# Cross-covariance attention with a highway layer: transposes of v in 32-bit words and by DMA, larger load groups, and a first chain that reads S in place

## The chip, the core and the metric

The kernel runs on one core of one Trainium2 chip. The metric is device time in microseconds (us), the median over runs; of the kernel before, three runs gave 270.11 us (270.1 to 270.67). A profile is one execution recorded by the hardware profiler. In it PE is TensorE (its matmuls), PEld its weight loads, DVE is VectorE, ACT is ScalarE, POOL is GpSimd and SP is SyncE.

## What is computed

`q`, `k`, `v` are four batches of 6336 rows by 256 channels in float32, and the output has the same 25344 x 256 values. Cut to what matters:

```python
qn = q / (np.linalg.norm(q, axis=1, keepdims=True) + 1e-06)     # norm of a channel over all 6336 rows
kn = k / (np.linalg.norm(k, axis=1, keepdims=True) + 1e-06)
s = kn.transpose(0, 2, 1) @ qn / tau                            # 256 x 256 per batch
a = np.exp(s - s.max(-1, keepdims=True)); a /= a.sum(-1, keepdims=True) + 1e-09
x = (v @ a).reshape(B * N, 256)
H = np.maximum(x @ w_h, 0.0)
T = 1.0 / (1.0 + np.exp(-(x @ w_t + b_t)))
out = T * H + (1.0 - T) * x
```

A batch's 256 x 256 matrix needs all rows of its q and k before the first row of its output can be made.

## The kernel before

**Tiles.** Of a batch's 6336 rows, 6272 are read as 49 tiles of 128 rows and the last 64 rows of all batches come as an extra tile ("rem"). GpSimd loads q, k and v in groups of several tiles (`QG`, `VG`; `load`, L177), cast to float16 on the way, into rings of 4 buffers for q, 4 for k and 3 for v. The very first four tiles of q and k come as float32 over SP and ACT and are cast by DVE and ACT (`cast_first`).

**Scores.** For each tile TensorE adds k^T q into the PSUM tile S (two matmuls of 256 columns, L230) and k^T k and q^T q, of which the diagonal is the squared norm, into G (two matmuls of 128 columns each, L234 and L239). For some runs of four tiles (`RUNS`) the squares are made instead by ACT (L449), POOL (L455) and DVE (L462), so those tiles need no G matmul. In the last `TAIL` tiles of a batch all of q's G matmuls come first, then k's, then S.

**The chain.** When a batch's scores are done, a chain of small steps makes its matrices (`make_chain`): norms from the diagonals (DVE, L503), roots, inverses, a copy of S from PSUM to SBUF on ACT (`ssb`, L520), the row `cq` of q's inverse norms spread over partitions by TensorE (L549), the product (DVE, L558), exp on ACT (L575), softmax (DVE, L589), a transpose (`at`, L600, copied at L611), and the products with w_h and w_t (`ah`, L619, copied at L630). Results lie side by side in `mr`: the attention matrix, and it times w_h and w_t. The chain of batch b runs while outputs of batch b-1 are being made; batch 0 has nothing to run beside it but the first scores of batch 1.

**Outputs.** The 25 pairs of tiles of each batch make 100 slots. A slot needs its v transposed: four TensorE transposes of 128 x 128 float16 into PSUM (`vtps`, L293) and one copy to SBUF (`vts`, L307) by DVE or ACT (`ACT_COPY`). Then come twelve matmuls of 256 columns at L317: four into `zbank` (the gate, onto a bias that ACT put there at L361), four into `h`, four into `x`. ACT makes the sigmoid `tt` (L358), DVE makes max(h,0)*tt (`o`, L366) and (tt-1)*x (`ux`, L376), POOL subtracts them (L399), and SP stores four slots at a time (L416).

**The order.** Every engine runs its instructions in order. The order is written by a planner inside the kernel: it steps through time with a length for each task, takes on each engine the first task of a list of queues that is ready, and emits it. Loads go out in the order of `order` when their buffer is free by the plan and at most `OUTST` are under way; stores are held back by `step_sp` while loads are waiting. `S_END` says by which slot the scores of the next batch are to be done.

Of the kernel before, what the change touches and what calls it, by code (L numbers as in the profile page):

```python
# [60 lines left out]
def kernel(  # L61
# [33 lines left out]
    QG = [spans(4, 8, 8, 8, 8, 8, 3, 2), spans(4, 4, 12, 12, 12, 5)]  # L95
    QG += [spans(4, 8, 12, 12, 8, 5)] * (B - 2)
    VG = [spans(4, 8, 12, 12, 13)] + [spans(12, 12, 12, 13)] * (B - 1)
    GT = {"q": 12, "k": 12, "v": 13}
    CH = 4
    SQR = {"q": 4, "k": 2}  # L100
    RUNS = {1: {'q': [4, 8, 20, 32, 36, 44], 'k': [0, 8, 24, 28, 32, 40]}, 2: {'q': [0, 8, 12, 16, 20, 24, 28, 36, 40], 'k': [0, 12, 16, 32, 40]}, 3: {'q': [8, 12, 20, 28, 32, 40, 44], 'k': [0, 8, 16, 28, 32, 36]}}
    TAIL = [6, 12, 10, 7]
    SPARE = 0
    QOFF, VOFF = [1.5, 3.0, 4.0, 0.5], [7.5, 3.5, 0.5, 9.5]
    SAHEAD = [0, 0.5, 10.0, 10.5]
    LOOKS = [3, 3, 2, 2]
    HOLD = [2, 1, 1, 5]
    DVE_SUBS = 3
    SINGLES = 8
    ACT_COPY = {3, 14, 21, 22, 26, 34, 36, 39, 40, 44, 45, 51, 53, 54, 58, 61, 63, 64, 72, 77, 81, 83, 84, 88, 91, 96, 98, 99}  # L110
    NEAR = 2
    OUTST = 7
    QRING, VRING, ORING = 4, 3, 7
    TTR, UXR, VTR = 4, 3, 5
    OG = 4
    LASTS_AT = 18
    LASTS = list(range(LASTS_AT)) + [NPAIR - 1] + list(range(LASTS_AT, NPAIR - 1))
    PAIRS = [list(range(NPAIR))] * (B - 1) + [LASTS]
    S_END = [21.5, 42.5, 65.0]
# [17 lines left out]
    for t in range(NSLOT):  # L137
        b, i = pair_of(t)
        if i % 2 == 1 and i < NPAIR - 1 and unit_of[t - 1][1] == 0 and t < NSLOT - SINGLES:
            pairsets[-1].append(t)  # L140
            unit_of[t] = (len(pairsets) - 1, 1)
        else:
            unit_of[t] = (len(pairsets), 0)
            pairsets.append([t])
# [9 lines left out]
    MM = lambda n: n / 2376.0 + 0.0025  # L154
    EXP_LAG = 0.6
    PE_LAG, LAG, TO_PE = 0.20, 0.08, 0.10
    TILE = 0.309
    STEP, LAND = 0.01, 0.9

# [10 lines left out]

    def load(kind, b, g):
        src = {"q": q, "k": k, "v": v}[kind]
        s0, ns = (VG if kind == "v" else QG)[b][g]
        ring = VRING if kind == "v" else QRING
        t = stream_pool.tile([P, GT[kind], C], f16, tag=f"{kind}_in", bufs=ring, name=f"{kind}{b}_{g}")
        tiles[kind, b, g] = t
        return nc.gpsimd.dma_start(out=t[:, 0:ns, :], in_=rows(src[b])[:, s0 : s0 + ns, :])  # L177
# [35 lines left out]
    S_t, G_t = {}, {}  # L213
# [5 lines left out]
    def emit_score(b, j, parts, first, last):  # L219
        if first:  # L220
            tags = ("S", "G") if b == 0 else ("hx1", "hx2")
            S_t[b] = psum_pool.tile([P, 2, C], f32, tag=tags[0], name=f"S{b}")
            G_t[b] = psum_pool.tile([P, 4, P], f32, tag=tags[1], name=f"G{b}")
        nr = REM if j == NS else P
        kk, qq = tile_of("k", b, j), tile_of("q", b, j)
        S, G = S_t[b], G_t[b]
        for c in range(2):
            kc = kk[0:nr, bass.ts(c, P)]
# [4 lines left out]
            if "k" in parts:  # L233
                nc.tensor.matmul(  # L234
                    G[:, c, :], kc, kc, start=begins(b), stop=False, skip_group_check=True,
                )
        for c in range(2 if "q" in parts else 0):
            qc = qq[0:nr, bass.ts(c, P)]
            nc.tensor.matmul(  # L239
                G[:, 2 + c, :], qc, qc, start=begins(b), stop=False, skip_group_check=True  # L240
# [4 lines left out]
    def begins(b):  # L245
        if b in begun:
            return False
        begun.add(b)
        return True
# [3 lines left out]
    def make_scores(b):  # L253
# [3 lines left out]
        for parts in "qks":  # L257
# [26 lines left out]
    vT_ps, vT_t = {}, {}  # L284
    slot_of = {pair_of(t): t for t in range(NSLOT)}

    def emit_transpose(t):
        b, i = pair_of(t)
        ps = psum_pool.tile([P, 2, 2, P], f16, tag="vT", name=f"vtps{t}")
        for u, r in enumerate(nrows(i)):  # L290
            vt = tile_of("v", b, 2 * i + u)
            for c in range(2):
# [3 lines left out]
        vT_ps[t] = ps  # L296

    def emit_copy(t, e):
        i = pair_of(t)[1]
        sb = work_pool.tile([P, 2, 2, P], f16, tag="vTs", bufs=VTR, name=f"vts{t}")  # L300
        cp = nc.vector.tensor_copy if e == "DVE" else nc.scalar.copy
        ps = vT_ps.pop(t)
        if i == NPAIR - 1:
            for u, r in enumerate(nrows(i)):
                cp(out=sb[:, u, :, 0:r], in_=ps[:, u, :, 0:r])
        else:
            cp(out=sb, in_=ps)  # L307
        vT_t[t] = sb
# [3 lines left out]
    def mains(t, dst, off, seeded):  # L312
        b, i = pair_of(t)
        mr = mr_t[b]
        for u, r in enumerate(nrows(i)):
            for kt in range(2):
                nc.tensor.matmul(  # L317
                    dst[0:r, u, :], vT_t[t][:, u, kt, 0:r], mr[:, kt, off : off + C],
# [14 lines left out]
    banks = [Bank("hx0")]  # L333
# [36 lines left out]

    def emit_ux(t):
# [10 lines left out]
    def out_tile(t):  # L382
# [3 lines left out]
        if i % OG == 0:  # L386
            o_t[b] = stream_pool.tile([P, 2 * OG, C], f32, tag="o", bufs=ORING, name=f"o{t}")
        return o_t[b], 2 * (i % OG)
# [43 lines left out]
    def make_run(kind, b, g, j):  # L432
# [37 lines left out]
        rd = Task(("red", kind, b, j), "DVE", 1.0, reduce, [(ad, LAG)])  # L470
        sq.after.append((task_of_load[kind, b, g], LAND))
# [21 lines left out]
    def make_chain(b):  # L493
        st = {}
        T = {}
        def norms(kind):
            def emit(e):
# [3 lines left out]
                for i in (o, o + 1):  # L501
                    junk = work_pool.tile([P, P], f32, tag="junk", bufs=1, name=f"junk{b}_{i}")
                    nc.vector.scalar_tensor_tensor(  # L503
                        out=junk, in0=G_t[b][:, i, :], scalar=0.0, in1=ident0,
# [4 lines left out]
        def pe_sums(e):  # L509
            for kind, o in (("q", 2), ("k", 0)):  # L510
                for c in range(2 if (kind, b) in sums_t else 0):
                    nc.tensor.matmul(
                        G_t[b][:, o + c, :],
                        areas[kind][sums_t[kind, b]][:, 0, bass.ts(c, P)], ones32,
# [3 lines left out]
        def ssb(e):  # L518
            st["ssb"] = work_pool.tile([P, 2, C], f32, tag="ssb", bufs=1, name=f"ssb{b}")
            nc.scalar.copy(out=st["ssb"], in_=S_t.pop(b))  # L520
# [35 lines left out]
        def logits(c):  # L556
            def emit(e):
                nc.vector.tensor_tensor(  # L558
                    out=st["ssb"][:, c, :], in0=st["ssb"][:, c, :], in1=st["cq"][:, 0, :],
# [4 lines left out]
        def exps(c):  # L564
            def emit(e):
# [3 lines left out]
                if c == 0:  # L569
                    st["e", c] = st["cq"][:, 1, :]  # L570
                elif T["exps", 1].bank is not None:
                    st["e", c] = bank_tile(T["exps", 1], f"e{b}")[:, 0, :]
# [71 lines left out]
        add("nq", "DVE", 0.7, norms("q"), after + [(grams[b, "q"], PE_LAG)])  # L644
        add("norms", "DVE", 0.7, norms("k"), after + [(grams[b, "k"], PE_LAG)])
        engine, length = ("ACT", 0.25) if b == 0 else ("POOL", 0.75)
        for kind, n in (("q", "nq"), ("k", "norms")):
            add(("root", kind), engine, length, root(kind), [(T[n], LAG)])
            if kind == "q":
                add("ssb", "ACT", 0.62, ssb, [(last_score[b], PE_LAG)])  # L650
# [4 lines left out]
        add("cq", "PE", 4 * MM(C), pe_cq, [(T["invs", "q"], TO_PE)],  # L655
            bank=lambda: [T["softmax", 0], T["logits", 1]])
        for c in range(2):
            add(("logits", c), "DVE", 0.38, logits(c), [(T["cq"], PE_LAG), (T["ssb"], LAG)])
            add(("exps", c), "ACT", 0.72, exps(c),
                [(T["logits", c], LAG), (T["invs", "k"], LAG)])  # L660

        T["exps", 1].may_bank = lambda: [T["softmax", 1]]
        back = lambda: add("back", "ACT", 1.5, lambda e: preload_table(Act.Sigmoid),
                           [(T["exps", 1], 0.0)])
        if b > 0:
            back()
# [5 lines left out]
        for c in range(2):  # L672
            add(("atc", c), "DVE" if c == 0 else "ACT", 0.4, at_copy(c), [(T["at", c], PE_LAG)])
            add(("ah", c), "PE", 2 * MM(2 * C), pe_ahat(c), [(T["atc", c], TO_PE)],
                bank=lambda c=c: [T["ahc", c]])
        for c in range(2):
            add(("ahc", c), "ACT" if c == 0 else "DVE", 0.62, ahat_copy(c),
                [(T["ah", c], PE_LAG)])
        if b == 0:
            back()  # L680
# [7 lines left out]
            "DVE.thux", "copy", "POOL.chain", "POOL.sub", "ACT.sq", "POOL.add", "DVE.red",  # L688
# [6 lines left out]
    order += [(-94.5, "remq", 0, 0), (-94.5, "remk", 0, 0)]  # L695
    order += [(-80, "q", 1, 0), (-80, "k", 1, 0), (-65, "q", 1, 1), (-65, "k", 1, 1)]
    order += [(-78, "w", 0, 0), (-78, "w", 0, 1)]
    order += [(-70, "v", 0, 0), (-69, "remv", 0, 0), (2, "remq", 0, 1), (2, "remk", 0, 1)]
# [20 lines left out]
    Z, H, X, TR, CP, TT, SEED, TH, UX, SUB = ({} for _ in range(10))  # L719
    for t in range(NSLOT):  # L720
# [15 lines left out]
        CP[t] = Task(("C", t), "any", 0.0, lambda e, t=t: emit_copy(t, e))  # L736
        TT[t] = Task(("tt", t), "ACT", 0.61, lambda e, t=t: emit_tt(t))
        SEED[t] = Task(("seed", t), "ACT", 0.61, lambda e, t=t: emit_seed(t))
        TH[t] = Task(("th", t), "DVE", 0.75 if odd else 0.61, lambda e, t=t: emit_th(t))
# [65 lines left out]
    zeros = const_pool.tile([P, 2 * C], f16, tag="zeros")  # L805
# [3 lines left out]
    def seed_banks():  # L809
        btp = psum_pool.tile([P, 2, C], f32, tag="hx0", name="btp")  # L810
# [39 lines left out]
    for b in range(2, B):  # L850
        score[b, 0].after += [(chains[b - 1]["norms"], TO_PE), (chains[b - 1]["ssb"], TO_PE)]

    for t in range(NSLOT):
        b, i = pair_of(t)
        m0, m1 = chains[b]["ahc", 0], chains[b]["ahc", 1]
        for task in (Z[t], H[t], X[t]):
            task.after += [(CP[t], TO_PE), (m0, TO_PE), (m1, TO_PE)]
# [4 lines left out]
        if t >= 1:  # L862
            TR[t].after.append((CP[t - 1], TO_PE))
        CP[t].after.append((TR[t], PE_LAG))
        if t >= VTR:
            CP[t].after.append((X[t - VTR], LAG))
# [3 lines left out]
        TH[t].after += [(H[t], PE_LAG), (TT[t], LAG)]  # L870
# [6 lines left out]
        if i < NPAIR - 1 and i % OG == 0:  # L877
            og = o_groups.index((b, i // OG))
            if og >= ORING:
                for s in store_of_group[o_groups[og - ORING]]:  # L880
                    TH[t].after.append((s.dma, LAG))
# [3 lines left out]
        queues["PE.T"].append(TR[t])  # L885
        queues["copy"].append(CP[t])
        queues["ACT.tt"].append(TT[t])
        queues["DVE.thux"] += [TH[t], UX[t]]
# [7 lines left out]
    for at, kind, b, g in order:  # L896
# [12 lines left out]
        ring = groups[kind]  # L909
        size = VRING if kind == "v" else QRING  # L910
        if len(ring) >= size:
            pb, pg = ring[-size]
            gs = (VG if kind == "v" else QG)[pb]
            lastj = gs[pg][0] + gs[pg][1] - 1
            if kind == "v":
                after.append((TR[slot_of[pb, lastj // 2]], PE_LAG + 0.2))
            else:
                after.append((score[pb, lastj], PE_LAG + 0.2))
        ring.append((b, g))
        gs = (VG if kind == "v" else QG)[b]  # L920
        add_load((kind, b, g), gs[g][1], lambda e, a=(kind, b, g): load(*a), after)
        if len(ring) > size:
            recycler[(kind,) + ring[-size - 1]] = loads[-1][0]

    for b in range(B):
        for i in range(NPAIR):
            for u in range(2):
# [3 lines left out]
                TR[slot_of[b, i]].after.append((d, LAND))  # L931

    for t in queues["PE.S"]:
        for kind, b, j in t.needs:
            d = task_of_load["rem" + kind, 0, min(b, 1)] if j == NS else \
                task_of_load[kind, b, group_of(QG[b], j)]
            t.after.append((d, LAND + (1.2 if b == 0 and j >= QG[0][-3][0] else 0.4 if b == 0 else 0.0)))
# [9 lines left out]
    log, ran = [], []  # L947

# [235 lines left out]
```

## Time and profile before

| | |
|---|---|
| median of three runs | 270.11 us |
| the profiled execution's own time | 270.2 us |
| its span, first to last instruction | 268.4 us |
| mean granted TensorE clock | 0.997 |
| busy: PE, PEld | 246.2 us, 213.9 us |
| busy: DVE, ACT, POOL | 207.8 us, 192.5 us, 205.3 us |
| bytes moved by the DMA engines | 66.08 MB |
| DMA busy, first 35 of 40 slices | 0.9 or more in 33 of them, 0.7 and 0.6 in the others |

The time of an execution is 1.8 us more than its span. [...] how fast matmuls follow each other is read from their start times in the timeline. The bytes of a load are counted as written, in float16, so 215 GB/s of loads is twice that read from memory.

### The profile page before, as it was taken

The numbers are of one execution on the slowest core, as the hardware profiler recorded it, in microseconds if no ns is written. First come the engines' busy times: TensorE is split into PE (matmuls) and PEld (weight loads), VectorE is DVE, ScalarE is ACT, GpSimd is POOL, SyncE is SP. The second block draws the span as 40 slices with busy tenths as digits, with TensorE's granted clock in tenths as the row PEclk, the third lists the DMA queues.
The fourth block names the chain that finished last, engine by engine and source line by source line (L and its number), as shares of the span: only waits on it lengthen the run. The fifth ranks groups of instructions, "written<-read, shape, count | busy, mean of one in ns | idle before, by whom it ended". The sixth has DMA issues, their size and how long they took to land.

```text
span 268.4 us, 6454 instructions
## 1 busy us (share of the span) xinstructions
PE 246.2 (92%) x2564; PEld 213.9 (80%) x2564; DVE 207.8 (77%) x415; ACT 192.5 (72%) x320; POOL 205.3 (76%) x182
## 2 busy tenths in 40 slices
PE   0996887899999999979999999999999999999991
PEld 0696785789989997869988987898989687989780
DVE  2000035869999999879989899899999998989895
ACT  3310026969689979869996798898867987888690
POOL 6133455489999999997899998899966485977870
PEclk9999999999999999999999999999999999999998
DMA  7999999999999999999999999999999999698436
GB/s 215 214 214 213 204 187 221 209 214 213 215 210 213 234 268 215 209 271 211 291 289 301 284 215 224 213 297 300 274 290 353 298 375 413 141 224 347 205 128 236
DMA packets 16287, 66.08 MB, mean 246 GB/s; under 512 B 1793, under 2 KB 4610, under 8 KB 13314
## 3 DMA queue, kind: packets, MB, share of 16 engines
q0 software_dynamic: 11040, 38.67, 73.2%
q1 hardware_dynamic: 4930, 26.35, 24.6%
q10 hardware_dynamic: 288, 0.66, 0.7%
q8 instruction: 20, 0.33, 0.4%
q14 instruction: 9, 0.07, 0.1%
HBM read 78.38 MB, written 25.95 MB: 389 GB/s over the span
## 4 chain that ended last, share of the span: by engine, by line
PE 39%; DMA 34%; POOL 10%; DVE 8%; issue 5%; ACT 3%; DVEq 0%; POOLq 0%; ACTq 0%
DMA k<-in_k_dram 19%; DMA v<-in_v_dram 10%; PE x L317 7%; PE zbank L317 7%; PE S L230 7%; PE h L317 7%; POOL o L399 5%; PE vtps L293 4%; DMA out_dram<-o 3%; PE G L234 3%; PE G L239 2%; DVE o L366 2%; DVE ux L376 2%; DMA qk<-in_k_dram 2%; ACT tt L358 1%
## 5 line engine op out<-in xcount | busy, mean ns | idle before, releaser
L399 POOL TENSOR_TENSOR o<-o,ux 128x1024 f32<-128x1024 f32 (+1 forms) x49 | 110.5, 2257 | 24.0 <-DVE ux L376 20.9
L317 PEld LDWEIGHTS <-vts 128*128 128x128 f16 x1200 | 111.7, 98 | 16.4 <-issue 4.3
L230 PE MATMUL S<-q,k 128*128 128x256 f16 x392 | 73.5, 278 | 13.0 <-DMA k<-in_k_dram 6.7
L358 ACT ACTIVATE tt<-zbank 128x512 f32<-128x512 f32 x100 | 59.3, 595 | 23.8 <-PE zbank L317 16.0
L366 DVE SCALAR_TENSOR_TENSOR o<-h,tt 128x512 f32<-128x512 f32 x96 | 65.8, 685 | 6.5 <-ACT tt L358 3.2
L376 DVE SCALAR_TENSOR_TENSOR ux<-tt,x 128x512 f32<-128x512 f32 (+1 forms) x104 | 68.1, 658 | 2.7 <-PE x L317 2.7
L317 PE MATMUL x<-mr,vts 128*128 128x256 f16 (+1 forms) x400 | 60.5, 273 | 0.4 <-DVE o L366 0.4
L317 PE MATMUL zbank<-mr,vts 128*128 128x256 f16 (+1 forms) x400 | 60.5, 273 | 0.0
L317 PE MATMUL h<-mr,vts 128*128 128x256 f16 (+1 forms) x400 | 60.5, 273 | 0.0
L361 ACT COPY zbank<-btb 128x512 f32<-128x512 f32 x98 | 57.6, 591 | 2.7
L230 PEld LDWEIGHTS <-k 128*128 128x128 f16 x392 | 37.6, 100 | 19.0 <-DMA k<-in_k_dram 7.9
L234 PE MATMUL G<-k 128*128 128x128 f16 x256 | 44.0, 224 | 0.7 <-DVE junk L503 0.7
L293 PE MATMUL vtps<-ident,v 128*128 128x128 f16 x392 | 38.3, 219 | 1.0 <-DVE vts L307 0.7
L307 DVE COPY vts<-vtps 128x512 f16<-128x512 f16 x68 | 28.6, 421 | 6.7 <-PE vtps L293 6.3
L293 PEld LDWEIGHTS <-v 128*128 128x128 f16 x392 | 28.7, 98 | 4.5 <-issue 1.7
L177 POOL DMA_DIRECT2D q<-in_q_dram x25 | 14.2, 568 | 23.1 <-PE G L239 18.6
L503 DVE SCALAR_TENSOR_TENSOR junk<-G,ident 128x128 f32<-128x128 f32 x16 | 4.7, 291 | 31.0 <-PE G L234 30.3
L239 PE MATMUL G<-q 128*128 128x128 f16 x216 | 28.6, 224 | 0.0
L455 POOL TENSOR_TENSOR sqq<-sqq 128x512 f32<-128x512 f32 (+1 forms) x22 | 26.4, 1204 | 0.1
L234 PEld LDWEIGHTS <-k 128*128 128x128 f16 x256 | 24.0, 101 | 1.8 <-issue 1.1
L449 ACT ACTIVATE sqq<-q 128x1024 f32<-128x1024 f16 x22 | 23.0, 1054 | 0.0
L462 DVE TENSOR_REDUCE sqq<-sqq 128x256 f32<-128x768 f32 x22 | 22.6, 1027 | 0.0
(78 smaller groups left out, 214.9 us busy)
## 6 DMA issues: line engine op xcount, KB each, us to landing
out_dram<-o SPq DMA_DIRECT2D x23, 1024.0 KB, 9.8
v<-in_v_dram POOLq DMA_DIRECT2D x11, 768.0 KB, 17.2
q<-in_q_dram POOLq DMA_DIRECT2D x7, 768.0 KB, 14.9
k<-in_k_dram POOLq DMA_DIRECT2D x7, 768.0 KB, 19.3
q<-in_q_dram POOLq DMA_DIRECT2D x9, 512.0 KB, 13.3
k<-in_k_dram POOLq DMA_DIRECT2D x9, 512.0 KB, 15.2
v<-in_v_dram POOLq DMA_DIRECT2D x4, 832.0 KB, 19.0
q<-in_q_dram POOLq DMA_DIRECT2D x4, 256.0 KB, 13.0
```

The source lines that it names most:

```text
L230: nc.tensor.matmul(S[:, c, :], kc, qq[0:nr, :], start=first and c == 0, stop=last and c == 1)
L234: nc.tensor.matmul(G[:, c, :], kc, kc, start=begins(b), stop=False, skip_group_check=True,)
L239: nc.tensor.matmul(G[:, 2 + c, :], qc, qc, start=begins(b), stop=False, skip_group_check=True)
L293: nc.tensor.transpose(ps[:, u, c, 0:r], vt[0:r, bass.ts(c, P)], ident[0:r, 0:r])
L307: cp(out=sb, in_=ps)
L317: nc.tensor.matmul(dst[0:r, u, :], vT_t[t][:, u, kt, 0:r], mr[:, kt, off : off + C], start=(not seeded and kt == 0 and (u == 0 or i == NPA ...
L358: nc.scalar.activation(out=tts[t], in_=zbank[t % 2], func=Act.Sigmoid)
L361: nc.scalar.copy(out=zbank[t % 2], in_=btb)
L366: nc.vector.scalar_tensor_tensor(out=ot[pr, o0 + us.start : o0 + us.stop, :], in0=hx["h", t][pr, us, :], scalar=0.0, in1=tts[t][pr, us, :] ...
L376: nc.vector.scalar_tensor_tensor(out=uxs[n][pr, 2 * half + us.start : 2 * half + us.stop, :], in0=tts[t][pr, us, :], scalar=1.0, in1=hx["x ...
L399: ins = sub.tensor_tensor(out=dst, in0=dst, in1=uxs[n][pr, us, :], op=AluOp.subtract)
L455: nc.gpsimd.tensor_tensor(out=sq[:, 1 : 1 + half, :], in0=sq[:, 1 : 1 + half, :], in1=sq[:, 1 + CH - half : 1 + CH, :], op=AluOp.add,)
```

## The change

Six things are changed, and the planner's constants with them, so that the order on every engine is another one.

1. **Load groups.** q and k come in groups of 6 to 17 tiles, 3 buffers each for q and k (before 3 to 12, after the first, and 4 buffers); v in groups of 1 to 13. In batch 0 the groups of q and k are 4, 16, 15 and 14 tiles, and the last 14 tiles have their q-diagonals, k-diagonals and S in that order (`TAIL`). There are 53 such loads; before there were 67.
2. **Late v in q's and k's buffers.** The last two groups of batch 3's v go to a buffer of q's ring and one of k's (`BORROW`).
3. **DMA transposes.** 22 of batch 3's 49 tiles of v (tiles 16 to 19, 24 to 35 and 42 to 47) are transposed by four DMA transposes on SP, behind the last load in the plan, into buffers of q's and k's rings, and used from there. They need no TensorE transpose and no copy.
4. **Words.** In batches 0 to 2 a float16 tile of 128 x 256 is seen as 128 x 128 words of 32 bits, and transposed by one float32 TensorE transpose in place of two float16 ones. The two halves of a word are channels 2i and 2i+1, so k's channels are taken even and odd, with a step of two elements, and the transposed v is read as weights with a step of two. One copy serves two slots (four tiles).
5. **First chain.** S is no longer copied; the product reads it from PSUM, and `cq` is copied to SBUF instead (`cqs`), in all four chains. In batch 0 q's diagonals have a PSUM bank of their own (`Gq`), ACT's table for the sigmoid is loaded right behind exp, and the engines of the last copies are chosen by `CENG`.
6. **Order.** Scores of batch 3 end at slot 69.5 of the plan (65 before), 40 runs of squares are made by ACT, POOL and DVE (39 before), and the loads ahead of the first slot are put in another order (`FIRSTS`).

The core of the diff:

```diff
-    QG = [spans(4, 8, 8, 8, 8, 8, 3, 2), spans(4, 4, 12, 12, 12, 5)]
-    QG += [spans(4, 8, 12, 12, 8, 5)] * (B - 2)
-    VG = [spans(4, 8, 12, 12, 13)] + [spans(12, 12, 12, 13)] * (B - 1)
+    QSZ = [[4, 16, 15, 14], [6, 10, 6, 14, 13], [14, 10, 12, 13], [16, 17, 16]]
+    VSZ = [[4, 1, 7, 12, 13, 12], [11, 6, 6, 13, 13], [13, 2, 3, 6, 13, 12], [6, 8, 8, 8, 6, 13]]
+    FIRSTS = ['remv', 'w', 'q10', 'v00', 'q11']
+    DT = [(16, 4), (24, 6), (30, 6), (42, 6)]
+    DT_FROM = 77
+    WORDS = [True] * (B - 1) + [not DT]
+    BORROW = {len(VG[B - 1]) - 2: "q", len(VG[B - 1]) - 1: "k"}
-    TAIL = [6, 12, 10, 7]
+    TAIL = [14, 12, 4, 4]
-    QRING, VRING, ORING = 4, 3, 7
-    TTR, UXR, VTR = 4, 3, 5
+    QRING, VRING, ORING = 3, 3, 7
+    TTR, UXR, VTU = 4, 3, 3
-    S_END = [21.5, 42.5, 65.0]
+    S_END = [22.0, 42.5, 69.5]
...
+    def channels(ap, kind, b, c):
+        if kind == "k" and words(b):
+            return ap.rearrange("p (i two) -> p two i", two=2)[:, c, :]
+        return ap[:, bass.ts(c, P)]
...
-            kc = kk[0:nr, bass.ts(c, P)]
+            kc = channels(kk[0:nr, :], "k", b, c)
...
+    def emit_dt(n):
+        s0, ns = DT[n]
+        kind = "qk"[n % 2]
+        g = group_of(VG[B - 1], s0)
+        o = s0 - VG[B - 1][g][0]
...
+        vt = stream_pool.tile([P, GT[kind], C], f16, tag=f"{kind}_in", bufs=QRING, name=f"vtd{n}")
+        ins = nc.sync.dma_start_transpose(
+            out=vt[:, 0:ns, :].rearrange("p s (c r) -> p (s c) r", c=2),
+            in_=tiles["v", B - 1, g][:, o : o + ns, :].rearrange("p s c -> p (s c)"),
+        )
...
             vt = tile_of("v", b, 2 * i + u)
-            for c in range(2):
+            if words(b):
+                nc.tensor.transpose(
+                    ps[:, u, 0:r], vt[0:r, :].bitcast(f32), ident0[0:r, 0:r]
+                )
+            for c in range(0 if words(b) else 2):
                 nc.tensor.transpose(
                     ps[:, u, c, 0:r], vt[0:r, bass.ts(c, P)], ident[0:r, 0:r]
                 )
...
+        vT_t[n] = sb.bitcast(f16).rearrange("p u (r c) -> p u c r", c=2) if words(b) else sb
...
-                    dst[0:r, u, :], vT_t[t][:, u, kt, 0:r], mr[:, kt, off : off + C],
+                    dst[0:r, u, :], vT_of(t, u)[:, kt, 0:r], mr[:, kt, off : off + C],
...
-        def ssb(e):
-            st["ssb"] = work_pool.tile([P, 2, C], f32, tag="ssb", bufs=1, name=f"ssb{b}")
-            nc.scalar.copy(out=st["ssb"], in_=S_t.pop(b))
+        def spread(e):
+            st["cqs"] = work_pool.tile([P, C], f32, tag="cqs", bufs=1, name=f"cqs{b}")
+            cp = nc.vector.tensor_copy if e == "DVE" else nc.scalar.copy
+            cp(out=st["cqs"], in_=st["cq"][:, 0, :])
...
-                    out=st["ssb"][:, c, :], in0=st["ssb"][:, c, :], in1=st["cq"][:, 0, :],
+                    out=st["ssb"][:, c, :], in0=S_t[b][:, c, :], in1=st["cqs"],
```

## The prediction

> **What bounds the kernel now.** I read the page's busy rows and slices first.
>
> ```profile
> PE 246.2 (92%) x2564; PEld 213.9 (80%) x2564; DVE 207.8 (77%) x415; ACT 192.5 (72%) x320; POOL 205.3 (76%) x182
> ...
> PE   0996887899999999979999999999999999999991
> ...
> DMA  7999999999999999999999999999999999698436
> ```
>
> DMA is full up to slice 34 (228 us), then has holes; PE is full nearly throughout. PE's record lengths overlap, so the timeline must say whether full is really full.
>
> ```profile
> 91.26 0.60 PE L317 MATMUL zbank<-mr,vts 128*128 128x256 f16 x4
> 91.70 0.60 PE L317 MATMUL h<-mr,vts 128*128 128x256 f16 x4
> 92.13 0.60 PE L317 MATMUL x<-mr,vts 128*128 128x256 f16 x4
> 92.57 0.82 PE L230 MATMUL S<-q,k 128*128 128x256 f16 x6
> 93.23 0.60 PE L317 MATMUL zbank<-mr,vts 128*128 128x256 f16 x4
> 93.66 0.61 PE L512 MATMUL G<-ones,sqq 128*128 128x128 f32 x4
> 94.11 0.61 PE L512 MATMUL G<-ones,sqk 128*128 128x128 f32 x4
> 94.56 0.39 PE L293 MATMUL vtps<-ident,v 128*128 128x128 f16 x4
> 94.78 0.60 PE L317 MATMUL h<-mr,vts 128*128 128x256 f16 x4
> ```
>
> From start to start, four float16 matmuls of 256 columns take 0.437 us (0.109 each), four of 128 columns 0.22 (0.055 each), four float32 records of 128 columns 0.45 (0.112 each). Nothing lies between. PE's whole work follows: 1200 output and 400 S matmuls at 0.109 are 174.4; 400 transposes, 488 G and 16 `at` at 0.055 are 49.7; 16 `ah` of 512 columns at 0.218 are 3.5; 40 float32 records at 0.112 are 4.5; setup 0.9. Sum 233.0 us. The first matmul starts at 6.3 us (PE's wait for the cast of k is 6.3 long), the last end is near 262.4. So 23 of 256 us are unfilled. The windows split it; bounds are the first `zbank` (45.7), the last chain's `cq` (205.5), and PE's end.
>
> ```profile
> 0.00:45.70 45.70, 33.39 (x360) 27.98 (x361) 6.89 (x30) 10.66 (x21) 18.64 (x38) 1.00 1.05 209
> 45.70:205.50 159.80, 156.46 (x1658) 138.63 (x1656) 144.94 (x275) 133.83 (x214) 145.28 (x119) 1.00 1.05 248
> 205.50:262.20 56.70, 55.94 (x550) 47.15 (x550) 52.74 (x107) 47.96 (x87) 41.40 (x25) 1.00 0.81 274
> 262.20:268.40 6.20, 0.40 (x4) 0.10 (x2) 3.21 (x6) 0.00 (x0) 0.00 (x0) 0.86 0.62 233
> ```
>
> By the same pricing of the instruction order, 27.4 us of PE's work lie before 45.7, so 12 us are unfilled there (loads and the first chain) and 10.6 after. The last window holds 52.9 of work in 56.7, with DVE busy 93%. After PE's end 6.2 us of last DVE work and stores follow. The waits say what the unfilled time is:
>
> ```profile
> PE S L230 <- DMA k<-in_k_dram: 6.7, 6, 1.6
> PE G L234 <- DVE junk L503: 0.7, 1, 0.7
> PE vtps L293 <- DVE vts L307: 0.7, 2, 0.5
> PE vtps L293 <- DMA v<-in_v_dram: 0.2, 1, 0.2
> ```
>
> Loads of k are most of it. After 45.7, gaps before k's S of 1.0 (at 52) and 1.8 us (at 115) are theirs; the other 7.7 are crumbs in which PE waits for a PSUM bank that DVE or ACT empties, or for a chain. v is hardly ever late. So from 45.7 on PE is the bound: an edit is worth the PE work it removes, plus the share of 7.7 us it closes.
>
> [...] Before has only packed weights; no run here shows a strided one. [...] float32 records follow at 112 ns, and their weight loads last 190 ns beside 98. [...] a float32 matmul is two records here, and no float32 transpose is in the trace. [...]
>
> **The change part by part.**
> *Transposes.* 150 float32 ones (batches 0 to 2) and 56 float16 ones (batch 3) stand for 400; DMA takes over 44. I take one record for a float32 one, [...] 0.112: 16.8 + 3.1 = 19.9 us against 22.0, 2.1 less. [...] I take 2.6. Bounds: at 0.055 each 8.5 less; at two records each, like the float32 matmuls, 16.8 more.
> *Strided operands* (`vts` as weights; k as weights and moving). Nothing if the load stays fast. [...] A gain has no cause.
> *DMA transposes.* 22 x 64 KB = 1.44 MB[...]. On SP they wait for their loads and for buffers of q and k; behind them stand the stores of the last 26 slots, and behind those DVE's `o`, but its 7 buffers hold 28 slots. The 6.5 MB of stores take 16 us at 413 GB/s, the page's best slice. The last v load of before is issued at 230.5 and lands 9.7 later, at 240; it moves seven slots earlier on POOL's queue, so loads end near 226. PE ends near 257 and first needs a DMA-transposed tile in slot 83, 23 us of its work before that: 234. So 8 us for the first of four and some 15 us for all cost nothing.
> *Squares.* One run more: 8 G matmuls, 0.4 us, go. ACT (1.05), POOL (1.2) and DVE (1.03) pay beside PE.
> *Copies.* DVE has 68 large copies of 0.42 (28.6). After: 20 of 128x512 words, 3 of 1024, some small. Priced as the float32 cast `mr`<-`ah` (0.69) and 0.8 they are 18: 10 less, of which 2 go back to three `cqs` copies (0.4) and a reduction (1.03). ACT: 16.3 + 2.3 (S) becomes 17 x 0.59 + 3 x 1.0 + 1 = 14. Both lie beside a full PE, so their worth is the crumbs: I take a third of 7.7, 2.6 us. If they were the bound, it would be up to 7.
> *Load groups.* Loads of 4, 8 and 12 tiles move in the same stream, 215 GB/s or 3.3 tiles of 64 KB per us, until 36 us; 14 fewer loads free 14 x 0.55 us of POOL, which is no bound, and a little DMA time, hidden behind PE after 45.7. In batch 0 they matter. The stream starts near 5.2, as the first float32 tiles land, and needs 1.2 to land, which fits k's last group (91.5 tiles at 3.25 per us: 33.4; issued 26.26, landed 8.4 later, 34.7). So 32 tiles land near 16.2, and PE, done with four tiles at 8, stands until 16; the next land at 25.5, the last k near 34.0, the two small groups' overhead gone. PE then has 28 G of k and 28 S: 1.5 + 3.1 + `cq` 0.45, S done at 39.2 against 38.5.
> *First chain.* The S copy (0.58) and the 0.72 wait of k's G for DVE go, the exp table is in by 38.4 (before 40.7). exp starts near 39.9 instead of 40.6. PE no longer stands 0.8 us before `at_1` for a load of k. The sigmoid table (1.28 + 0.2) now stands ahead of the first copy of `at` on ACT, and both `ahc` (0.69) on DVE. First `zbank` 45.1: 0.6 earlier. In later batches S's bank is free one product later, and outputs fill PE meanwhile. But k's second group of batch 1 (about 133 tiles down the queue, 48.6 us) holds PE 1 to 1.7 us at 47. Net zero.
> *Late v, later S_END.* v made PE wait 0.2 us; nothing. The last chain starts at slot 70.7, not 66, with 8.6 us of PE work before slot 75 against some 8.4 of chain: no loss, no margin.
>
> Sum: transposes -2.6, G -0.4, crumbs -2.6, start 0: -5.6. Span 268.4 - 5.6 = 262.8; with the 1.8 around it, 264.6 us. The profiled 270.2 is the median's 270.11 within 0.1.
>
> **Rivals.**
> *Strided operands lose the fast load (slower):* L230/L234 in batches 1 and 2[...]. It decides once each of 132 pairs costs over 42 ns more. For: no strided row in the trace. [...] A two-record transpose would be 281.
> *DMA transposes hold the stores:* past 15 us for 44 blocks of 128x128 (0.34 each) every us adds one; it decides at 21 us (0.47), and 0.6 gives 276. [...]
> *Coarser groups eat the gain:* only PE's 3.0 us go, the crumbs stay, and the wait at 47 costs 1.2 net: 268.4 - 3.0 + 1.2 + 1.8 = 268.4. For: groups of 13 to 17 land whole, with one buffer less. Against: the two waits for k after 45.7 are all before has.
> *Transposes at 0.055:* another 8 us: 256.6. Against: the 190 ns load.
> *Load groups do nothing:* v was never late and DMA never the bound after 45.7; that is inside the main sum.
>
> **How the numbers follow.** Main case 0.58 (264.6, own range 261.5 to 267.5), transposes cheap 0.10, coarse groups 0.14, strided or two-record 0.12, DMA transposes 0.06. Faster: 0.58 + 0.10 + 0.09; same 0.05 (0.2%, or 0.5 us, is about what a measurement of this kernel tells from no change); slower 0.12 + 0.06. The range 258 to 272 leaves out half of the cheap, half of the strided and all of the last: 0.17.
>
> **What would show it.** Float32 `vtps` records: starts 0.11 apart and one each (right), 0.055 or two each (wrong). Weight loads of `vts` at 98 ns, G of k still 0.055 after S. First `zbank` near 45. PE's unfilled time after it near 8 us. DVE copies near 18 us. The last DMA transpose landing before slot 97 and stores not queueing behind it. The prediction is wrong if PE stops being full, above all before S in 20 to 60 us and near slot 75, or if the last us are a queue of stores.

## The result, and the profile after

The changed kernel takes 269.81 us (median of 20 runs, 269.19 to 272.01), the kernel before 270.93 us in the same comparison (20 runs, 270.1 to 272.4). The ratio is 0.9966, with a 95% interval of 0.9948 to 0.9985: faster by a third of a per cent. The prediction had 264.6 us. The sign and the range (258 to 272) held; some four fifths of the forecast gain of 5.5 us did not come. Ratios compare the fast executions of each kernel alone, while medians also count the few that took over 1.5% longer than its fastest, so the two can differ a little.

The profiled execution took 269.51 us, its span 267.7. First the busy rows, the slices of PE and DMA and the DMA queues on the page of the kernel after:

```profile
PE 243.9 (91%) x2362; PEld 211.6 (79%) x2362; DVE 203.3 (76%) x370; ACT 190.1 (71%) x314; POOL 199.7 (75%) x170
...
PE   0869998899999996999999989999999989999990
...
DMA  7999999999999999999999999999999999999466
...
q0 software_dynamic: 9024, 38.67, 71.6%
q1 hardware_dynamic: 10690, 27.79, 28.0%
```

PE's row has lost 202 records, and DVE's and ACT's rows are shorter, as forecast. But PE's slices show new dents, and DMA is at nine tenths or more from slice 2 to slice 37. The last two lines are what the prediction passed over: the packets of the two main queues together took 99.6% of 16 engines' span. On the page of the kernel before the same two lines read:

```profile
q0 software_dynamic: 11040, 38.67, 73.2%
q1 hardware_dynamic: 4930, 26.35, 24.6%
```

That is 97.8%. By this count the DMA engines had hardly more air than PE already before the change. The count adds up the packets' own time, and in the windows below it passes 1, so it does not say by itself that nothing more fits; how much it held back is measured by the experiments with fewer stores. The change makes loads cheaper (73.2% of 268.4 is 196.5 us, 71.6% of 267.7 is 191.7) and adds the DMA transposes to the other queue (66.0 to 75.0 us).

The windows of the kernel after, cut at its first `zbank` (44.75), its last chain (217.5) and PE's end:

```profile
0.00:44.75 44.75, 33.80 (x348) 28.32 (x349) 6.80 (x30) 10.98 (x21) 13.12 (x28) 1.00 1.02 213
44.75:217.50 172.75, 167.53 (x1623) 147.87 (x1623) 153.92 (x263) 141.04 (x227) 152.22 (x120) 1.00 1.04 260
217.50:261.70 44.20, 42.62 (x395) 35.36 (x392) 39.97 (x74) 38.12 (x67) 34.39 (x24) 1.00 0.91 264
261.70:267.70 6.00, 0.00 (x0) 0.00 (x0) 2.66 (x6) 0.00 (x0) 0.00 (x0) 0.65 0.67 231
```

In the middle window PE is not busy for 5.2 of 172.75 us; in the kernel before it was 3.3 of 159.8. With every matmul priced by the pace from start to start, as in the prediction, PE's work fell from 232.9 to 230.1 us, and what is unfilled between its first and last matmul rose from 23.7 to 25.1. So the last matmul starts 1.3 us earlier (261.0 for 262.3). The tail behind it is 0.6 longer (6.7 for 6.1), half of it in the last store, which ends 3.3 us after its issue starts in place of 2.9. The span is 0.7 shorter.

The waits of the kernel after between 45.7 and 240 us (total, times, longest) say where PE stands now:

```profile
PE at L705 <- DVE mr L694: 2.2, 1, 2.2
...
PE S L262 <- DMA k<-in_k_dram: 1.3, 2, 1.1
...
PE vtps L376 <- DVE vts L400: 1.2, 1, 1.2
```

The same view of before has these lines:

```profile
PE S L230 <- DMA k<-in_k_dram: 2.5, 2, 1.6
PE x L317 <- DVE o L366: 0.4, 1, 0.4
PE cq L549 <- DVE inv L543: 0.4, 1, 0.4
PE ah L619 <- DVE o L366: 0.2, 1, 0.2
PE vtps L293 <- DVE vts L307: 0.2, 1, 0.2
```

The loads of k at 52 and 115 us (2.5 us) are no longer waited for; the one at 46.9 us, which the prediction foresaw, is. In the view of after the first and the third line are new, and both lead to one kind of operation. Here is the timeline of VectorE, GpSimd and PE around the first of them, other lines left out:

```profile
99.79 2.36 POOL L503 TENSOR_TENSOR o<-o,ux 128x1024 f32<-128x1024 f32 x1
...
101.02 3.18 DVE L694 TENSOR_SCALAR mr<-ssb,rinv 128x256 f16<-128x256 f32 x1
...
102.10 1.93 POOL L559 TENSOR_TENSOR sqq<-sqq 128x256 f32<-128x256 f32 x2
...
104.25 0.28 PE L705 MATMUL at<-ident,mr 128*128 128x128 f16 x2 [2.20 <-DVE mr L694]
104.30 0.35 DVE L694 TENSOR_SCALAR mr<-ssb,rinv 128x256 f16<-128x256 f32 x1
```

The scaling of exp by 1/sum lasts 3.18 us and ends at 104.20, just after GpSimd's run of three operations (104.03). PE stands still for 2.36 us by its start times; the view, which counts from the end of a record, says 2.20. The same scaling right after it, with GpSimd idle, lasts 0.35. All eight of after, grouped by what they read, and behind them those of before that read SBUF:

```profile
L694 DVE TENSOR_SCALAR mr<-ssb,rinv x5: 353/354/3179, 101.0 to 219.0; 128x256 f16<-128x256 f32 x5
...
L694 DVE TENSOR_SCALAR mr<-e,rinv x3: 483/484/485, 41.2 to 218.5; 128x256 f16<-128x256 f32 x3
```

```profile
L589 DVE TENSOR_SCALAR mr<-ssb,rinv x2: 767/812/858, 102.5 to 159.7; 128x256 f16<-128x256 f32 x2
```

The three numbers are the shortest, the median and the longest in ns. `ssb` lies in SBUF, `e` in PSUM. Those from PSUM take 484 ns. Of those from SBUF three took 353 or 354 with GpSimd idle, but two took 3.18 and 2.48 us beside its operations. In before, six of the eight read PSUM, 484 ns each, the ones at 159.1, 208.3 and 208.8 us beside a GpSimd operation. The change had moved the first half of exp out of `cq`'s bank, to a free bank or else to SBUF.

### The profile page after: what moved, and what is told of

It reads as the page before. It is cut to its first block, busy times and chain, and to the rows that moved or that the text cites. A ratio compares the mean times of both kernels' runs of the same rounds, so it can differ in the third digit from the quotient of the medians.

```text
span 267.7 us, 5994 instructions
## 1 busy us (share of the span) xinstructions
PE 243.9 (91%) x2362; PEld 211.6 (79%) x2362; DVE 203.3 (76%) x370; ACT 190.1 (71%) x314; POOL 199.7 (75%) x170
## 3 DMA queue, kind: packets, MB, share of 16 engines
q0 software_dynamic: 9024, 38.67, 71.6%
## 4 chain that ended last, share of the span: by engine, by line
PE 60%; DMA 26%; DVE 7%; POOL 2%; ACT 2%; issue 1%; DVEq 0%; POOLq 0%
DMA k<-in_k_dram 24%; PE zbank L410 13%; PE x L410 13%; PE h L410 12%; PE S L262 10%; PE vtps L376 4%; PE G L266 3%; DVE mr L694 2%; PE G L271 2%; DMA qk<-in_k_dram 2%; DVE o L459 1%; DVE ux L478 1%; PE ah L724 1%; PE G L616 1%; PE vtps L380 1%
## 5 line engine op out<-in xcount | busy, mean ns | idle before, releaser
L410 PEld LDWEIGHTS <-vts 128*128 128x128 f16 (+1 forms) x1068 | 101.6, 98 | 17.7 <-issue 6.0
L478 DVE SCALAR_TENSOR_TENSOR ux<-tt,x 128x512 f32<-128x512 f32 (+2 forms) x104 | 68.0, 657 | 1.7 <-PE x L410 1.6
L410 PE MATMUL zbank<-mr,vts 128*128 128x256 f16 (+1 forms) x356 | 54.1, 273 | 0.7 <-DVE mr L735 0.7
L410 PE MATMUL h<-mr,vts 128*128 128x256 f16 (+1 forms) x356 | 53.9, 273 | 0.2 <-DVE o L459 0.2
L410 PE MATMUL x<-mr,vts 128*128 128x256 f16 (+1 forms) x356 | 53.9, 273 | 0.0
L376 PE MATMUL vtps<-ident,v 128*128 128x128 f32 x147 | 26.2, 275 | 1.2 <-DVE vts L400 1.2
L559 POOL TENSOR_TENSOR sqk<-sqk 128x512 f32<-128x512 f32 (+1 forms) x20 | 24.0, 1199 | 1.1 <-ACT sqk L553 1.0
L197 POOL DMA_DIRECT2D v<-in_v_dram x23 | 12.9, 564 | 12.1 <-PE vtps L376 9.8
L271 PEld LDWEIGHTS <-q 128*128 128x128 f16 x232 | 19.9, 102 | 2.2
L566 DVE TENSOR_REDUCE sqk<-sqk 128x256 f32<-128x768 f32 x20 | 20.6, 1029 | 1.1 <-POOL sqk L559 1.1
## 6 DMA issues: line engine op xcount, KB each, us to landing
k<-in_k_dram POOLq DMA_DIRECT2D x3, 896.0 KB, 23.7
v<-in_v_dram POOLq DMA_DIRECT2D x3, 768.0 KB, 21.1
```

What stands on the lines that cost most here:

```text
L271: nc.tensor.matmul(Gq[:, c, :], qc, qc, start=begins(b, "q"), stop=False, skip_group_check=True)
L376: nc.tensor.transpose(ps[:, u, 0:r], vt[0:r, :].bitcast(f32), ident0[0:r, 0:r])
L410: nc.tensor.matmul(dst[0:r, u, :], vT_of(t, u)[:, kt, 0:r], mr[:, kt, off : off + C], start=(not seeded and kt == 0 and (u == 0 or i == NP ...
L478: nc.vector.scalar_tensor_tensor(out=uxs[n][pr, 2 * half + us.start : 2 * half + us.stop, :], in0=tts[t][pr, us, :], scalar=1.0, in1=hx["x ...
L559: nc.gpsimd.tensor_tensor(out=sq[:, 1 : 1 + half, :], in0=sq[:, 1 : 1 + half, :], in1=sq[:, 1 + CH - half : 1 + CH, :], op=AluOp.add,)
```

## The experiments

Theory A, the first: a scaling that reads exp from SBUF stands until the GpSimd operations beside it end (3.18 and 2.48 us above), one that reads PSUM does not (484 ns), and that ate the gain. That a form which also sums its row would not stand either was the author's guess; no run had shown it. Rival B: another wait (loads in coarse groups, chains without margin) limits, and takes over if this one goes. Rival C: it is the second input, `rinv`, that makes the scaling stand, not its form. Times are medians, ratios are to the kernel before on the same chip.

**The scaling in a form that also sums its row (`a_accum`), after's order kept.**

```
-  scalar1=rinv, scalar2=None, op0=mult, op1=bypass)
+  scalar1=rinv, scalar2=0.0,  op0=mult, op1=add, accum_out=rs[c])
```

> After with one instruction form changed and every engine's order kept: the scaling of exp by 1/sum (L694) also sums its row[...]. Theory A [...] two of them stand 3.18 and 2.48 us until a GpSimd operation ends. Then here all of them take 0.45 to 0.6 us, PE's waits for mr in the chain near 101 us (2.4) and for the vts copy near 157 us (1.3) go, and the median falls by 2.7 to 3.4 us, to 266.4 to 267.1. Rival B (tight chains and coarse load groups): what PE waits for there is the chain's place and the loads; another wait takes over, and the median stays within 0.4 us of after's 269.8. Rival C [...]: the two scalings stay at 2 to 3 us and the time stays.

Measured: 270.42 us, ratio 0.9985 (0.9963 to 1.0007). The scaling's group of this run (TENSOR_SCALAR_CACHE_REDUCE is the accumulating form), and four of its waits between 45.7 and 240 us:

```profile
L694 DVE TENSOR_SCALAR_CACHE_REDUCE mr<-ssb,rinv x5: 479/479/479, 101.1 to 219.7; 128x256 f16<-128x256 f32 x5
```

```profile
ACT sqq L553 <- DMA q<-in_q_dram: 3.3, 1, 3.3
...
PE vtps L376 <- DMA v<-in_v_dram: 2.0, 3, 1.1
...
PE S L262 <- DMA k<-in_k_dram: 1.5, 2, 1.3
...
PE vtps L376 <- ACT vts L400: 0.8, 1, 0.8
```

What A forecast for the scalings came: with no other edit, all five from SBUF take 479 ns, in the place of those of 3.18 and 2.48 us too, and PE's waits for `mr` (2.2 us) and for the copy behind it (1.2) are gone. Why this form does not stand is not shown. C falls, since `rinv` is still read from SBUF. Yet the time did not fall as A said (266.4 to 267.1). PE arrives earlier and stands for v (2.0 us) and for a copy that ACT delays while it stands 3.3 us for a load of q. Rival B is nearer with the time, 0.6 us above after where it allowed 0.4. What was open then is why the loads are late.

**Exp's first half in PSUM again (`a_psum`), planned anew.**

```
-  add("cq", ..., bank=lambda: [T["cqs"]])
+  add("cq", ..., bank=lambda: [T["cqs"], T["softmax", 0]])
-  st["e", 0] = a free bank, or ar[:, 0, :]
+  st["e", 0] = st["cq"][:, 1, :]
```

> After with the first half of exp written into the second half of cq's PSUM bank, as in before; the planner plans anew with that bank held longer, so the order of many instructions moves. Theory A: four of eight scalings surely read PSUM at 0.48 us; a long one (over 1 us) is left only where a second half lies in SBUF beside a GpSimd operation, as in before (0.77 and 0.86); the median falls by 2 to 3.4 us, to 266.4 to 267.8. Rival B: within 0.6 us of 269.8, either sign, since loads and chains stand as in after. Rival C: as A, since rinv is the only SBUF input left.

Measured: 271.62 us, 1.0029 (1.0014 to 1.0044). One scaling of a second half from SBUF still lasts 2.59 us, and PE stands 1.9 us for a load of v at 180 us. The gain that A forecast is missed again, and B's range (within 0.6 us of 269.8) too; the order is a new one here, so the 1.2 us above `a_accum` is not traced further.

**Before with exp's first half in SBUF (`b_sbuf`), order and banks kept.**

```
-  st["e", 0] = st["cq"][:, 1, :]
+  st["e", 0] = ar[:, 0, :]
```

> Before with the first half of exp written back over its logits in SBUF, in place of cq's PSUM bank; the order on every engine and all banks are kept. Theory A: the scalings of the first half in batches 1 and 2 (at about 102 and 159 us) now [...] last until its operation ends, 1 to 3 us in place of 0.484; those beside an idle GpSimd take 0.35. The median rises by 1 to 4 us, to 271.9 to 274.9 beside 270.9. Rival B: where exp lies doesn't matter, 270.5 to 271.3.

Measured: 273.56 us, 1.0081 (1.0056 to 1.0106), 2.2 us slower by the ratio. The group of the scaling, from a profiled execution that took 275.59 us, longer than most of this kernel's:

```profile
L589 DVE TENSOR_SCALAR mr<-ssb,rinv x6: 354/1260/2025, 41.5 to 211.2; 128x256 f16<-128x256 f32 x6
```

So where exp lies does cost, in the kernel where nothing else was touched, and as much as forecast. At 102.3 us one lasted 1.46 us while GpSimd did no arithmetic but issued three loads (102.01 to 103.66), and it ended at 103.77: a long one was seen beside load issues as well.

**Half of the stores left out: `a_half`, `a_accum_half`, `b_half`.** In batches 0 to 2 only the first half of each output group is stored, so that part of the output is missing; orders are kept. It relieves the DMA engines, and with `a_accum` it makes a square of two causes. (Output buffers come free sooner too, but in after PE waits only 0.2 us for one.) Theory D: from 45 us on the scalings that stand beside GpSimd, which stop PE for 2.36 and 1.34 us in after, and full DMA engines hold PE in turn.

```
-  lo, hi = (0, 2 * n)
+  lo, hi = (0, 2 * n if b == B - 1 else n)
```

> After with only the first half of each output group of batches 0 to 2 stored (18 groups, 1.05 MB each: 9.4 of 25.4 MB of stores, some 24 of 267 us of DMA engine time, less); the order on every engine is kept, the rest of the output is left out. Theory D: from 45 us on two things set PE's pace in turn[...]; take one away and the other fills most of what it left. [...] less DMA brings little: 0.5 to 1.5 us, 268.3 to 269.3. Rival E (DMA alone sets the pace): 3 to 5 us less, 264.8 to 266.8. Rival F (DMA doesn't matter, PE's copies and chains do): 269.4 to 270.2.

> Both at once: [...] half of the stores of batches 0 to 2 left out. Theory D: with both gone the waits for late q, k and v at 145, 151 and 181 us (1.0, 0.6, 1.2) and those behind them go too: 265.3 to 267.3, that is 3 to 5 us below a_accum's 270.4, more than a_half gains on after. Rival E: 264.8 to 266.8 and equal to a_half. Rival F: 269.8 to 270.8, as a_accum.

> Before with the same half of the stores of batches 0 to 2 left out, the order kept. Before's DMA engines are full until 220 us too. Theory D: the late k at 115 us (1.8), and q and k at 155 and 182 (0.5 each) go: 1.5 to 3 us less than 270.8, 267.8 to 269.3. Rival F: 270.4 to 271.2.

| | all stores | half of the stores |
|---|---|---|
| before | 1 (270.7 us) | 0.9908 (0.9889 to 0.9927), 268.06 us |
| after | 0.9966 (0.9948 to 0.9985) | 0.9952 (0.9930 to 0.9973), 269.24 us |
| after, accumulating scaling | 0.9985 (0.9963 to 1.0007) | 0.9804 (0.9785 to 0.9822), 265.32 us |

Taken alone, neither cause is worth anything that shows in after: 0.9966 goes to 0.9952 or to 0.9985. Both together bring 1.6%, some 4.4 us. That is D; its rivals E (DMA alone sets the pace) and F (DMA does not matter) fall. First `a_half`: its PE slices, its granted clock, its DMA slices, and (a second view) two of its waits:

```profile
PE   0767998999999996999999989999999989999990
...
PEclk9999999999999997999999999999999999999996
DMA  7999999999999999999999982679999669997357
```

```profile
PE at L705 <- DVE mr L694: 2.2, 1, 2.2
...
PE vtps L376 <- DVE vts L400: 1.3, 1, 1.3
```

The DMA engines now have holes (slices of 2 and 6), but PE's waits for the scaling and for the copy behind it stand as in after. The first of them even cost more here. Behind its stop of 2.4 us PE ran at half clock for 3.4 us (granted 0.50 from 104.1 to 107.5, the 7 in slice 16): the nine S matmuls that follow took 2.13 us, the same nine in after, behind a stop as long, 1.15. That is some 1.6 us of this profiled execution, which at 270.70 us is near the top of the kernel's 268.06 to 271.01; how many of the others had it is not known. So waits that take turns need not be all of the joint effect: here the clock fell behind such a stop as well. In `a_accum_half`, whose clock has no such dip, the middle stretch is full; here is its window, and below it that of `a_accum` for the same stretch:

```profile
45.70:200.00 154.30, 153.51 (x1493) 135.93 (x1492) 137.68 (x239) 131.48 (x210) 140.16 (x112) 1.00 1.00 225
```

```profile
45.70:200.00 154.30, 149.45 (x1448) 131.38 (x1447) 133.24 (x232) 128.24 (x205) 135.84 (x107) 1.00 1.04 249
```

PE is busy 4.1 us more, with 45 more matmuls done by 200 us, and the only load that PE still waits for after 45.7 is k, 0.2 us. PE's unfilled time between first and last matmul falls from 26.2 to 21.1 us.

`b_half` gives the measure of the change itself. Its unfilled time is 21.1 us too, the same as `a_accum_half`'s, and 23.7 in before: the late k at 115 us (1.8) is gone. Its two scalings from SBUF still stand,

```profile
L589 DVE TENSOR_SCALAR mr<-ssb,rinv x2: 832/1552/2271, 102.6 to 156.5; 128x256 f16<-128x256 f32 x2
```

and the longer one costs PE 0.6 us at 158.6, through the copy of `at` that is queued behind it on VectorE. So with the DMA engines relieved and hardly a wait for a scaling left on PE's path, before and after differ by 2.7 us (268.06 and 265.32), which is about PE's 2.8 us of removed work; no other gain of the change shows.

**Without DMA transposes (`a_dt_off`)**, batch 3 planned anew; and the same with the accumulating scaling (`a_nodt_accum`).

```
-  DT = [(16, 4), (24, 6), (30, 6), (42, 6)]
+  DT = []
```

> After without the DMA transposes: PE transposes the last 22 tiles of v too, in words, 22 records more at 0.109 us (2.4 us, in a stretch in which PE is full), with 11 pairs to copy on VectorE or ScalarE; the planner plans batch 3 anew. By the prediction's sum 2.4 us are lost: 271.5 to 273. Theory D adds nothing to that, since these transposes run from 229 to 238 us, when the loads are almost done. If instead their 9.0 us of DMA engine time delay the stores at the end, this gains: 268 to 269.5.

> After without DMA transposes [...]. The first added 1.6 to 2.2 us to after, by PE's 22 more records. If theory D holds [...]: 270.6 to 272.0. If the DMA transposes' own 9 us of DMA time were what kept a_accum from gaining, it now gains 2 us or more: 268 to 269.5.

Measured: `a_dt_off` 271.40 us, 1.0033 (1.0017 to 1.0048); `a_nodt_accum` 271.48 us, 1.0025 (1.0014 to 1.0035). Against after the first loses 0.7%, 1.8 us, a little less than the 2.4 us of PE work that comes back. The DMA transposes are worth their place: their 9 us of DMA time fall where the loads end. And the accumulating scaling gains nothing here either (1.0025 beside 1.0033), so they are not what kept `a_accum` from gaining.

**Words off (`a_words_off_accum`)**, from `a_accum`, planned anew.

```
-  WORDS = [True] * (B - 1) + [not DT]
+  WORDS = [False] * B
```

> a_accum with the words off: batches 0 to 2 transpose v by four float16 records for a pair in place of two float32 ones; the planner plans anew. By the prediction's prices: 150 records at 0.112 against 300 at 0.055 are equal (16.8 and 16.5)[...]; ACT's copies of a pair of slots take 1.0 in place of 0.59. If the words save PE time, this is 1.5 to 2.5 us above a_accum; if they only make the copies cheaper, PE's work is the same within 0.5 us and the median is 0 to 1 us above a_accum.

Measured: 276.29 us, 1.0194 (1.0150 to 1.0237), 2.1% above `a_accum`. Both readings were too low. ACT has 23 large copies of 1.01 us in place of 17 of 0.59 and three of 1.01, and is busy 200.3 us for 190.4; PE's unfilled time is 33.0 us, with waits for late k (2.3), late v (2.1) and one for `o` (2.1). In the profiled execution (mean granted clock 0.970) two stops are each followed by 3.4 us at half clock (from 146.8 and 228.7), which by an estimate from half the pace is 3.4 us lost. How much of the 5.9 us is ACT's load and how much the new order and its clock is not separated.

**Smaller first groups (`a_nodt_small_first`)**, planned anew, against `a_dt_off`.

```
-  QSZ = [[4, 16, 15, 14], ...
+  QSZ = [[4, 10, 12, 12, 11], ...
```

> a_dt_off (271.4) with batch 0's loads of q and k in groups of 4, 10, 12, 12 and 11 tiles in place of 4, 16, 15 and 14; the planner plans anew. The prediction held that the group of 16 costs nothing at the start, since k's last tile lands at 34 us either way. If so, PE's standstill of 3.8 us at 11.6 us shrinks, [...] and the first zbank still comes within 0.6 us of 44.7; the median 270.8 to 272.2. [...] If smaller groups with three buffers each hold the load stream up, it comes 1 to 3 us later: 272.5 to 275.

Measured: 276.70 us, 1.0205 (1.0160 to 1.0250). PE's standstill of 3.8 us at 11.6 becomes two, 1.1 at 10.6 and 4.5 at 16.3; the first `zbank` comes at 45.8 in place of 44.4, and later waits are longer (2.3 us at 133, 1.9 in the last chain), and again two stretches of 3.4 us ran at half clock (from 135.6 and 224.4; mean granted clock 0.969). The last reading is nearest, with the first `zbank` 1.4 us later, but the time lies above its range. Smaller groups with three buffers each bring nothing; the size of the loss belongs in part to the new order and its clock.

**A trial at a faster version (`a_nodt_replan4`, `a_nodt_replan2`)**: the accumulating scaling without DMA transposes, and settings that the planner's own model prefers once a store costs it 7.5% more.

```
-  s.units = ... 2 * n
+  s.units = ... 2.15 * n
-  HOLD = [2, 1, 1, 4]
+  HOLD = [2, 0, 0, 7]      # replan4; replan2: [1, 0, 0, 2]; lead times, squares and copies too
```

> A trial at a faster version without DMA transposes: [...] the planner's settings searched anew with stores priced 7.5% dearer, as they went on the chip (store holds, load lead times, places of the square runs, who copies). If the late loads come from the order of loads and stores, 267.5 to 269.3; if the sum of DMA work holds the middle whatever the order, 270 to 272.

> A second, different result of that search. The same two readings: 267.5 to 269.3, or 270 to 272.

Measured: 288.25 us, 1.0622 (1.0566 to 1.0678), and 278.87 us, 1.0248 (1.0173 to 1.0323). Both readings missed, in both. Two waits of the first, around 132 us:

```profile
DVE o L459 <- DMA out_dram<-o: 6.6, 1, 6.6
...
PE x L410 <- DVE o L459: 6.3, 1, 6.3
```

Stores that go later in favour of loads keep the output buffers, and PE stands behind the buffer; in the second such waits for `o` come to 6.1 us, the longest 2.8. Nothing here beats after among kernels that write the whole output.

## Why the prediction was right and wrong

Its sum was -5.6 us of span: transposes -2.6, G -0.4, crumbs -2.6, start 0. The span fell by 0.7: PE's work -2.8 and not -3.0, its unfilled time +1.4 and not -2.6, the tail +0.6 and not 0 (these add up to the 0.7 within 0.1). The sign was earned by PE's removed work. That the time fell into the range is owed to the range, which was made wide enough for rivals; the main case's own, 261.5 to 267.5, was missed.

*Transposes and squares: right.* Four float32 records in after's timeline (the middle line):

```profile
72.57 0.38 PE L262 MATMUL S<-q,k 128*128 128x256 f16 x2
72.79 0.60 PE L376 MATMUL vtps<-ident,v 128*128 128x128 f32 x4
73.22 0.60 PE L410 MATMUL zbank<-mr,vts 128*128 128x256 f16 x4
```

They take 0.43 us, 0.108 each, one record for a transpose; the median from one to the next is 0.111 over the run. At 0.110, 150 of these and 56 at 0.055 are 19.6 us against 22.0, which is 2.4 less (2.6 forecast: 2.1 at 0.112 each, the rest the author's estimate), and the 8 G are 0.4. That is the 2.8 by which PE's whole work fell. The rival with 0.055 each is out, and no further gain shows. The price was right; what sets it is not shown: the weight loads' own records last 141 ns, and 190 for the float32 matmuls, which follow at 0.112.

*Strided operands: right.* Weight loads of `vts` still last 98 ns, those of k 101 to 102 (100 to 101 before), and G of k still follows at 0.055. The rival that these operands would cost did not happen; what it would cost was the author's estimate.

*DMA transposes: right that they are hidden.* SP issued them from 228.8 to 241 us, they landed a median of 5.2 us after their issue, and PE, which used them from 237.0 on, waited for one 0.2 us in `a_accum` and not at all in after. No run had shown their rate; measured, their packets took 9.0 us of the DMA engines for 1.44 MB, 160 GB/s.

*Start: right.* First `zbank` 44.8, its second matmul 45.35, predicted 45.1; the standstill until 15.5 at the 16-tile group was there, and the first `zbank` came as predicted all the same. The wait for k at 46.9 was 1.26 us (1 to 1.7 predicted), and two others for k went.

*Copies: the step that failed.* It read 7.7 us of PE's unfilled time after 45.7 as waits for PSUM banks that DVE or ACT empties, or for a chain, and took a third, 2.6 us, for lighter copies. The copies did become lighter (DVE's of `vts` 16.5 us, from 30.6), but no such gain shows: with the DMA engines relieved and PE's waits for scalings down to 0.6 us in the one and none in the other, before and after leave 21.1 us unfilled alike. The view of before that is shown above could have said so. It has 0.8 us of waits for `o` and `vts`, and 0.4 for a step of the chain. A good part of the rest is no wait at all. PE does the outputs of the last 64 rows with weights of 64 columns, and each of these 12 groups of four matmuls takes 0.65 us from start to start of the next in place of 0.437, in before and in after: 2.6 us that no copy can fill. What the copies are worth alone stays open, since `a_words_off_accum`, with heavier ones, had a new order as well.

*Load groups: the second failed step.* "A little DMA time, hidden behind PE after 45.7" took PE as the bound and DMA as slack. The slices in the prediction's own first block said otherwise: DMA at nine tenths up to slice 34. `b_half` measures what the DMA engines held back in before: 0.9% for 9.4 MB less to store.

*First chain: the third.* "In later batches S's bank is free one product later, and outputs fill PE meanwhile ... Net zero" left out where exp goes. Reading it from SBUF cost PE 2.36 us at 101.8 and, through the copy queued behind it on DVE, 1.34 at 156.8, 3.7 in all. By itself such a move costs 2.2 us (`b_sbuf`); in after it hides the DMA limit, and the DMA limit hides it.

*Last chain: a term mis-sized.* "No loss, no margin" became 1.5 us of waits for `at_sb` and `ah` at 219 to 221 us, where before had 0.7 at 210 to 211: ACT's first copy stands behind the sigmoid table, which it loads from 218.3 to 219.6 us.

The rival "coarser groups eat the gain" had 268.4 us, the nearest figure, but its mechanism (groups land whole, with a buffer less) is not what was found: in `a_accum_half` the groups and buffers are the same, and with less to store the loads come in time. The lateness is the DMA engines' sum of work. Whether the limit lies in these engines or in the memory behind them, these runs do not tell.

## What to carry to other kernels

Here two resources stood above nine tenths (PE at 92%, the DMA queues at 98% before the change), and of two limits in the kernel after, neither showed when it was relieved alone: the other took its place. Relieve both, alone and together, before calling a cause absent. Add up the DMA queues' shares on the page before calling an engine the bound. Before taking a share of unfilled time as a gain, name what fills it, wait by wait. And when an edit moves an operand from PSUM to SBUF, price the instruction that reads it beside the work of the other engines at that time, not by its old duration: here 0.35 us beside an idle GpSimd, up to 3.18 beside a busy one.

## What the runs showed of the hardware

- A 128x256 `tensor_scalar` from float32 to float16 on VectorE took 484 ns from PSUM, with GpSimd idle or busy; from SBUF 353 with GpSimd idle and up to 3179 with it busy; and 479 from SBUF in the accumulating form, in all five places of `a_accum`. The longest, from 101.02 to 104.20 us, lasted past three GpSimd operations (to 102.15, the other two to 104.03), and one of 1.46 us in `b_sbuf` stood beside load issues. From SBUF with GpSimd idle it took 0.13 us less than from PSUM, and once 2.7 more.
- Float32 transposes of 128x128 were one record each and followed each other at 0.108 to 0.111 us, with weight loads of 141 ns, where the float32 matmuls of before had loads of 190.
- Four float16 matmuls of 256 columns took 0.65 us when two of them have weights of 64 columns, 0.437 when all have 128.
- Some stops of PE were followed by 3.4 us at half clock (granted 0.50 in `a_half`): one of 2.4 us in `a_half` (101.8), one of 2.2 in `a_words_off_accum` (144.3). One of 2.4 in after (101.8) and one of 3.0 in `a_nodt_replan2` (128.6) were not. What decides it these runs do not show. In after, float16 matmuls of 128 columns follow at 0.107 instead of 0.055 from the first ones at 6.7 us on until 21.1, with a standstill of 3.8 us among them; the granted clock of that stretch reads 1.00, so it does not account for this pace. In `a_words_off_accum` the last chain leaves PE almost idle from 224.4 to 228.5, and behind it these groups of four start 0.85 us apart in place of 0.437:

```profile
229.15 1.06 PE L410 MATMUL h<-mr,vts 128*128 128x256 f16 x4
230.00 1.06 PE L410 MATMUL x<-mr,vts 128*128 128x256 f16 x4
```
